# The last chunk's output product in three accumulators instead of one

## The chip, the cores and the metric

The kernel runs on one core of a Trainium2 chip. The metric is the time of one execution on the device in microseconds (us); the time of a kernel is the median of several runs. A profile is taken from one further execution. Its "span" is the time from the first to the last recorded instruction, and its own time is a little longer than its span.

## The reference

Per head, a 40x40 state is carried through 768 tokens, and each token reads it before it is updated. The 3072 rows that come out (4 batches of 768 tokens, 8 heads of 40 side by side make 320 columns) go through a feed-forward layer with a squared ReLU:

```python
for t in range(S):
    y[:, :, t] = einsum('bhd,bhde->bhe', rt, state)
    Sa = einsum('bhde,bhe->bhd', state, at)
    state = state * wt[:, :, None, :] - einsum('bhd,bhe->bhde', Sa, bt) + einsum('bhd,bhe->bhde', vt, kt)
x = y.transpose(0, 2, 1, 3).reshape(3072, 320)
h = x @ w_in                   # 320 -> 2048
g = maximum(h, 0) ** 2
out = g @ w_out                # 2048 -> 320
```

## The kernel before

**Chunks.** The 768 tokens are cut into 12 chunks of 64. For each chunk c the kernel loads its slices, prepares decay factors, solves the recurrence inside the chunk, carries the state on, reads it out, turns the result so that features lie on partitions (XT), and runs the feed-forward layer on the chunk's 4 x 64 = 256 rows. Matmul inputs are bf16; products are accumulated in PSUM as fp32.

**Feed-forward of one chunk (function ffn).** The hidden layer has 16 blocks of 128 features, handled in four groups u of four blocks. For each group the matmuls "F" and "FL" fill a PSUM tile, "f" applies the ReLU on its way to the SBUF buffer G (two buffers, chunk c uses G[c % 2]), and "q" squares it in place, on VectorE (DVE), ScalarE (ACT) or GpSimd (POOL). Then the output product "O" runs over the same 16 blocks j. The chunk's 256 rows are two row groups g of 128. For one j and one g, one matmul takes 128 columns of G as weights (128x128) and the 320 columns of WOUT[:, j] as moving data, and adds into columns 0 to 319 of half g of one PSUM tile. Each half is 512 fp32 wide. A chunk has 16 x 2 = 32 such matmuls, in four steps "O c u0" to "O c u3"; step u needs the squares of groups 0 to u.

**The ordinary chunk** is then copied out of PSUM to the SBUF buffer osb in one instruction ("o c", 128x640), and two DMAs on SyncE's queue (SP) store it, one for each pair of batches ("st c", line 947).

**The last chunk (c = 11)** is handled apart. Its last step u3 is split into "OL 11 g1" and "OL 11 g0": four matmuls for row group 1, then four for row group 0. Four copies follow, each 128x160: for g = 1 and then g = 0, columns 0 to 159 on ACT ("o0", line 374) and columns 160 to 319 on DVE ("o1", line 369). Four DMAs (line 960) store 63 rows each: for each g, one ("st0") on SP's queue and one ("st1") on ACT's queue. It has 63 rows instead of 64, since the output is shifted by one token.

**What sets the order.** A plan records every operation with what it reads and writes; the order itself is written out by hand in the string ORDER (lines 87 to 215), which names the engine, the PSUM slot (PE0 to PE3; four slots of two 2 KiB banks each) and the operation. Operations are issued in that order, each engine works its own queue in order, and the waits between engines are put in by the framework from the tiles and the regions that the instructions touch. The end of ORDER is:

```python
u3; ACT q 11 u3; PE2 O 11 u0; DVE o 10; PE O 11 u1; SP st 10; PE O 11 u2; PE OL 11 g1; PE OL 11
g0; ACT o0 11 g1; DVE o1 11 g1; ACT o0 11 g0; DVE o1 11 g0; ACT st1 11 g0; ACT st1 11 g1; SP st0
11 g1; SP st0 11 g0"""
```

In the instruction list of the kernel the waits of these last instructions are: the first copy (ACT, g1) waits for PE; each of the other three copies waits for the copy before it on the other engine, although it reads other columns; a store waits for the copies of its own g only. Line 388 is the helper that issues every ordinary matmul, line 395 the one for whole 128x128 transposes, lines 369 and 374 the copies on DVE and ACT; lines 908, 914, 916 and 918 are the ReLU on ACT and the squares on DVE, POOL and ACT; lines 947 and 960 are the output stores.

Of the kernel before, what the change touches and what calls it, by code (L numbers as in the profile page):

```python
# [7 lines left out]
FP32 = mybir.dt.float32  # L8
# [201 lines left out]
ACT f 10 u2; DVE f 10 u1; PE1 F 11 u2; ACT q 10 u2; DVE q 10 u1; PE0 FL 11 u1; PE2 FL 11 u3; DVE q  # L210
10 u0; PE FL 11 u2; PE FL 11 u0; PE F 11 u3; ACT f 11 u0; PE F 11 u1; ACT f 11 u2; PE3 O 10 u0;
ACT q 11 u2; PE O 10 u1; ACT f 11 u1; PE O 10 u2; ACT f 11 u3; POOL q 11 u1; ACT q 11 u0; PE O 10
u3; ACT q 11 u3; PE2 O 11 u0; DVE o 10; PE O 11 u1; SP st 10; PE O 11 u2; PE OL 11 g1; PE OL 11
g0; ACT o0 11 g1; DVE o1 11 g1; ACT o0 11 g0; DVE o1 11 g0; ACT st1 11 g0; ACT st1 11 g1; SP st0
11 g1; SP st0 11 g0"""


@with_exitstack
def kernel(
# [13 lines left out]
    NB, NHH, T, D = r.shape  # L233
    L = 64
    NCH = T // L
# [4 lines left out]
    DM = moe_w_in.shape[0]  # L240
# [85 lines left out]
    def slot(h, dt):  # L326

        if h not in slots:
            i = plan.slot_of[h]
            slots[h] = ps.tile([128, 2, 512 if dt == FP32 else 1024], dt, name=f"pb{i}",  # L330
                               tag=f"pb{i}", bufs=1)
        return slots[h]
# [8 lines left out]
    def pe(name, mode, cols, mms, **kw):  # L341

        d = {"R": max(28.6, cols / 2.4 + 1) / 2, "Q": max(31.0, cols / 2.4 + 1) / 2,
             "C": max(31.0, cols / 2.4 + 1) / 2,
             "D": max(22 if cols < 64 else 60.6, cols / 2.4 + 2.5)}[mode]
        plan.add(name, [("PE", d * len(mms))], ("pe", d, mms), mode=mode, n_mm=len(mms), **kw)

    def ew(name, alts, **kw):
        plan.add(name, [(e, d) for e, d, _ in alts], ("ew", {e: f for e, d, f in alts}), **kw)
# [14 lines left out]
    def copy_alts(o_, i_, n, fast=False, scale=None, engines=("DVE", "ACT")):  # L364
        alts = []
        if "DVE" in engines:
            if scale is None:
                alts.append(("DVE", c_dve(n, fast),
                             lambda: nc.vector.tensor_copy(out=o_(), in_=i_())))  # L369
            else:  # L370
                alts.append(("DVE", c_dve(n), lambda: nc.vector.tensor_scalar(  # L371
                    out=o_(), in0=i_(), scalar1=scale, scalar2=None, op0=ALU.mult)))
        if "ACT" in engines:
            alts.append(("ACT", c_act(n), lambda: nc.scalar.activation(  # L374
                out=o_(), in_=i_(), func=ACTF.Copy, scale=1.0 if scale is None else scale)))
        if "POOL" in engines:
            alts.append(("POOL", 190 + 0.83 * n,
                         lambda: nc.gpsimd.tensor_copy(out=o_(), in_=i_())))  # L378
        return alts
# [493 lines left out]
    def ffn(c):  # L873
        q2 = c % 2
        for u in range(NFB // 4):
            hf = ("F", c, u)
            tail = u % 2 == 1
            ms = []
            for rg in range(2):
                for i in range(2):  # L880
                    for k2 in range(2):
                        ms.append(mm(
                            lambda rg=rg, i=i, hf=hf: slot(hf, FP32)[:, rg, NT * i:NT * i + NT],
                            lambda rg=rg, k2=k2, i=i, u=u: WIN[
                                :, k2, 512 * u + 256 * rg + 128 * i:
                                512 * u + 256 * rg + 128 * i + 128],
                            lambda k2=k2: XT[q2][:, k2, :],
                            i == 0 and k2 == 0 and not tail, k2 == 1 and tail))
            wide = dict(reads=[("XT", q2), ("WIN", 0, u), ("WIN", 1, u)], writes=[hf],
                        alloc=[] if tail else [hf])  # L890
            ml = []
            for i in range(2):
                for rg in range(2):
                    ml.append(mm(
                        lambda rg=rg, i=i, hf=hf: slot(hf, FP32)[:, rg, NT * i:NT * i + NT],
                        lambda rg=rg, i=i, u=u: WLAST[
                            rows(rg), u, 128 * i:128 * i + 128],
                        lambda rg=rg: XT[q2][rows(rg), 2, :], i == 0 and tail, not tail))
            last = dict(reads=[("XT", q2), ("WLAST",)], writes=[hf], alloc=[hf] if tail else [])
            for x in (1, 0) if tail else (0, 1):  # L900
                if x:
                    pe(f"FL {c} u{u}", "R", NT, ml, **last)
                else:
                    pe(f"F {c} u{u}", "D", NT, ms, **wide)
            gv = G[q2][:, 4 * u:4 * u + 4, :].rearrange("p j t -> p (j t)")
            gb = G[q2][:, 4 * u:4 * u + 4, :].rearrange("p (s j) t -> p s (j t)", s=2)
            ew(f"f {c} u{u}", [
                ("ACT", c_act(1024), lambda gb=gb, hf=hf: nc.scalar.activation(  # L908
                    out=gb, in_=slot(hf, FP32)[:], func=ACTF.Relu)),
                ("DVE", c_dve(1024), lambda gb=gb, hf=hf: nc.vector.tensor_scalar(  # L910
                    out=gb, in0=slot(hf, FP32)[:], scalar1=0.0, scalar2=None, op0=ALU.max))],
               reads=[hf], writes=[("G", q2, u)], free=[hf])
            ew(f"q {c} u{u}", [
                ("DVE", 690, lambda gv=gv: nc.vector.tensor_tensor(
                    out=gv, in0=gv, in1=gv, op=ALU.mult)),
                ("POOL", 1900, lambda gv=gv: nc.gpsimd.tensor_tensor(  # L916
                    out=gv, in0=gv, in1=gv, op=ALU.mult)),
                ("ACT", c_act(1024), lambda gv=gv: nc.scalar.activation(  # L918
                    out=gv, in_=gv, func=ACTF.Square))],
               reads=[("G", q2, u)], writes=[("G", q2, u)])  # L920
        ho = ("O", c)
        for u in range(NFB // 4):
            ms = [[], []]
            for j in range(4 * u, 4 * u + 4):
                for g in range(2):
                    ms[g].append(mm(
                        lambda g=g: slot(ho, FP32)[:, g, 0:DM],
                        lambda g=g, j=j: G[q2][:, j, 2 * g * L:2 * g * L + 2 * L],
                        lambda j=j: WOUT[:, j, :], j == 0, j == NFB - 1))
            rd = ([("G", q2, x) for x in range(max(u, O_AFTER) + 1)]  # L930
                  + [("WOUT", 2 * u), ("WOUT", 2 * u + 1)])
            if c == NCH - 1 and u == NFB // 4 - 1:

                for g in range(2):
                    pe(f"OL {c} g{g}", "D", DM, ms[g], reads=rd, writes=[ho + (g,)])
            else:
                pe(f"O {c} u{u}", "D", DM, [m for x in zip(*ms) for m in x], reads=rd,
                   writes=[ho, ho + (0,), ho + (1,)], alloc=[ho] if u == 0 else [])
        ov = out.rearrange("(g bb s) f -> bb s g f", g=2, bb=2)
        t0, n = c * L + 1, min(L, T - 1 - c * L)  # L940
        if c < NCH - 1:
            ew(f"o {c}", copy_alts(lambda: osb[q2][:], lambda: slot(ho, FP32)[:, :, 0:DM], 2 * DM),
               reads=[ho, ho + (0,), ho + (1,)], writes=[("osb", q2)], free=[ho])

            def store():
                for bb in range(2):
                    nc.sync.dma_start(out=ov[bb, t0:t0 + n], in_=osb[q2][64 * bb:64 * bb + n])
            plan.add(f"st {c}", [("SP", 1500)], ("ew", {"SP": store}), reads=[("osb", q2)],
                     writes=[("left", c)])
            return  # L950
        h = DM // 2
        for g in range(2):
            for x, e in enumerate(("ACT", "DVE")):
                ew(f"o{x} {c} g{g}", copy_alts(
                    lambda g=g, x=x: osb[q2][:, g, h * x:h * x + h],
                    lambda g=g, x=x: slot(ho, FP32)[:, g, h * x:h * x + h], h, engines=(e,)),
                   reads=[ho + (g,), ("left", c - 2)], writes=[("osb", q2, g, x)], free=[ho])
            for bb, (e, q) in enumerate((("SP", nc.sync), ("ACT", nc.scalar))):
                plan.add(f"st{bb} {c} g{g}", [(e, 750 if e == "SP" else 60)],
                         ("ew", {e: lambda q=q, bb=bb, g=g: q.dma_start(  # L960
                             out=ov[bb, t0:t0 + n, g], in_=osb[q2][64 * bb:64 * bb + n, g])}),
                         reads=[("osb", q2, g, 0), ("osb", q2, g, 1)])

    def weights():

# [97 lines left out]
```

## Time and profile before

| | |
|---|---|
| median of 3 runs | 250.95 us (249.91 to 251.05) |
| the profiled execution's own time | 249.74 us |
| its span | 248.0 us |
| mean granted TensorE clock | 0.987 of full speed |
| TensorE (PE) busy | 223.8 us, 90% of the span |
| VectorE (DVE) busy | 189.1 us, 76% |
| ScalarE (ACT) busy | 178.0 us, 72% |
| GpSimd (POOL) busy | 110.1 us, 44% |

How to read the views used below. A row of a timeline has the start in us from the span's start, the length in us, the engine, the line, the operation, what it writes and reads, the count of instructions merged in it, and in brackets how long the engine had been idle and what released it. In the chain of waits each row is a piece of the one chain that ended last: start, length, engine and line. A row of the groups has the count, the busy time in us, the mean of one in ns, and the idle time before. PE is the matmul itself and PEld the weight load, which has a row of its own. SPq and ACTq are the issue of DMAs by those engines; a DMA's transfer goes on after its issue has ended. The page also cuts the span into 40 slices of 6.2 us; each digit is the busy share of a slice in tenths.

### The profile page before, as it was taken

The page shows a single profiled execution, that of the slowest core. Times are in us where ns is not written, and L with a number is a line of the kernel's source. Part 1 is how long each engine was busy: PE and PEld are TensorE (multiplying, and loading weights), DVE is VectorE, ACT ScalarE, POOL GpSimd, SP SyncE. Part 2 cuts the span into 40 slices and gives each one's busy share as a digit, 9 for nine tenths or more (in the row PEclk, how much of TensorE's full clock was granted, in tenths as well). Part 3 has the DMA queues.
Part 4 walks back from the last instruction along what each step waited for, and adds up shares of the span by engine and source line. Part 5 has one row for each costly group of instructions (what it writes and reads, how often), then busy time and mean ns, then how long its engine had stood idle before and what let it go on. Part 6 is the DMA issues. An engine that isn't in the chain of part 4 may idle for free.

```text
span 248.0 us, 12188 instructions
## 1 busy us (share of the span) xinstructions
PE 223.8 (90%) x5568; PEld 177.3 (71%) x5568; DVE 189.1 (76%) x236; ACT 178.0 (72%) x236; POOL 110.1 (44%) x110
## 2 busy tenths in 40 slices
PE   0588677599999999999999999999999999999991
PEld 0377666488787877788878877877788787867770
DVE  7698988359987889898869696999897578854411
ACT  2588889569899687868777887774777773944850
POOL 4144024532765716473870991491279900033030
PEclk9999999979999999999999999999999999999997
DMA  5989899989999969769698099995410000302021
GB/s 131 209 216 206 168 200 259 328 145 214 181 215 207 152 150 168 138 128 181 136 183 166 14 219 152 193 176 119 119 47 3 3 5 15 96 5 56 0 50 55
DMA packets 102152, 33.54 MB, mean 135 GB/s; under 512 B 88918, under 2 KB 101718, under 8 KB 101846
## 3 DMA queue, kind: packets, MB, share of 16 engines
q1 hardware_dynamic: 101958, 32.62, 63.0%
q8 instruction: 43, 0.70, 1.3%
q10 hardware_dynamic: 144, 0.16, 0.2%
q14 instruction: 7, 0.06, 0.1%
HBM read 28.84 MB, written 3.93 MB: 132 GB/s over the span
## 4 chain that ended last, share of the span: by engine, by line
PE 74%; DVE 9%; DMA 6%; ACT 4%; issue 3%; POOL 1%; SPq 1%; ACTq 0%
PE pb L388 63%; PE pb L392 7%; PE pb L395 4%; DMA G<-in_moe_w_in_dram 3%; DVE KBT L510 2%; DMA raw_a<-in_a_dram 2%; DVE AR L643 1%; DMA out_dram<-osb 1%; POOL WIN L378 1%; ACT G L908 1%; DVE STb L318 1%; DVE VU L371 1%; DVE lo L384 1%; DVE EN L669 1%; ACT osb L374 1%
## 5 line engine op out<-in xcount | busy, mean ns | idle before, releaser
L388 PE MATMUL pb<-WOUT,G 128*128 128x320 bf16 x384 | 57.1, 299 | 0.0
L916 POOL TENSOR_TENSOR G<-G 128x1024 bf16<-128x1024 bf16 x19 | 36.2, 1913 | 39.7 <-PE pb L392 19.3
L388 PE MATMUL pb<-XT,WIN 128*128 128x256 bf16 x384 | 49.9, 279 | 0.0
L908 ACT ACTIVATE G<-pb 128x1024 bf16<-128x1024 f32 x37 | 37.4, 1022 | 14.3 <-PE pb L388 13.1
L388 PEld LDWEIGHTS <-G 128*128 128x128 bf16 x384 | 35.9, 98 | 13.8 <-issue 0.5
L388 PEld LDWEIGHTS <-WIN 128*128 128x128 bf16 x384 | 35.6, 99 | 8.0 <-issue 2.6
L669 DVE TENSOR_TENSOR CX<-pb,MSKI 128x1024 bf16<-128x1024 f32 x24 | 28.9, 1220 | 12.1 <-PE pb L388 11.9
L382 POOL TENSOR_TENSOR KB<-raw_kb,iG 128x640 bf16<-128x640 f32 x14 | 21.6, 1542 | 24.3 <-ACT iG L553 19.9
L669 DVE TENSOR_TENSOR EN<-pb,MSK 128x1024 bf16<-128x1024 f32 x24 | 29.1, 1217 | 3.2 <-PE pb L388 3.1
L559 ACT ACTIVATE Gin<-pb 64x320 f32<-64x320 f32 x48 | 20.2, 428 | 9.4 <-PE pb L388 8.9
L378 POOL CAST VU<-raw_v 64x640 bf16<-64x640 f32 x20 | 14.3, 713 | 16.0 <-DMA raw_v<-in_v_dram 15.6
L761 DVE TENSOR_TENSOR STb<-pb,GT 64x640 bf16<-64x640 f32 x22 | 18.1, 820 | 1.4 <-PE pb L388 0.8
L388 PEld LDWEIGHTS <-EN 64*64 64x64 bf16 x768 | 14.5, 110 | 5.8 <-issue 4.8
L918 ACT ACTIVATE G<-G 128x1024 bf16<-128x1024 bf16 x17 | 17.7, 1055 | 0.1
L643 DVE TENSOR_TENSOR AR<-pb,GT 128x512 bf16<-128x512 bf16 x24 | 15.6, 683 | 2.7 <-PE pb L395 1.7
L374 ACT ACTIVATE osb<-pb 128x640 f32<-128x640 f32 (+1 forms) x10 | 6.2, 623 | 15.2 <-PE pb L388 14.7
L910 DVE TENSOR_SCALAR G<-pb 128x1024 bf16<-128x1024 f32 x11 | 13.4, 1222 | 4.7 <-PE pb L388 4.1
L388 PE MATMUL pb<-XT,WLAST 64*128 64x256 bf16 x192 | 16.8, 271 | 0.0
L382 POOL TENSOR_TENSOR lo<-lnW,hi 128x640 bf16<-128x640 f32 x6 | 8.9, 1492 | 15.8 <-ACT hi L374 10.3
L388 PE MATMUL pb<-hi,UTI 64*128 64x320 bf16 x48 | 7.9, 325 | 7.9 <-DVE hi L369 7.9
L839 DVE TENSOR_TENSOR Yb<-pb,Gin 128x128 bf16<-128x128 f32 (+1 forms) x24 | 12.4, 549 | 2.5 <-PE pb L388 2.3
L374 ACT ACTIVATE AR<-pb 128x512 bf16<-128x512 bf16 x19 | 10.6, 595 | 5.2 <-PE pb L392 3.6
(112 smaller groups left out, 447.1 us busy)
## 6 DMA issues: line engine op xcount, KB each, us to landing
raw_w<-in_w_dram SPq DMA_DIRECT2D x24, 160.0 KB, 4.3
raw_a<-in_a_dram SPq DMA_DIRECT2D x24, 160.0 KB, 4.1
raw_kb<-in_b_dram SPq DMA_DIRECT2D x24, 160.0 KB, 4.1
raw_kb<-in_k_dram SPq DMA_DIRECT2D x24, 160.0 KB, 4.2
raw_v<-in_v_dram SPq DMA_DIRECT2D x24, 160.0 KB, 5.4
raw_r<-in_r_dram SPq DMA_DIRECT2D x22, 160.0 KB, 5.2
out_dram<-osb SPq DMA_DIRECT2D x22, 160.0 KB, 3.1
osb<-in_moe_w_out_dram SPq DMA_DIRECT2D x8, 320.0 KB, 4.8
```

The source lines that it names most:

```text
L374: alts.append(("ACT", c_act(n), lambda: nc.scalar.activation(out=o_(), in_=i_(), func=ACTF.Copy, scale=1.0 if scale is None else scale)))
L378: lambda: nc.gpsimd.tensor_copy(out=o_(), in_=i_())))
L382: return [("POOL", 40 + 2.35 * n, lambda: nc.gpsimd.tensor_tensor(out=o_(), in0=a_(), in1=b_(), op=op)), ("DVE", c_dve(n), lambda: nc.vect ...
L388: return lambda: nc.tensor.matmul(out=o_(), lhsT=l_(), rhs=r_(), start=start, stop=stop, skip_group_check=True)
L392: return lambda: nc.tensor.transpose(out=o_(), in_=i_(), identity=IDb[rows(g), :])
L559: nc.scalar.activation(out=Gin[c % NGI][rows(g), NP * jh:NP * jh + NP, :].rearrange("p j e -> p (j e)"), in_=slot(hb, FP32)[rows(g), g, 0: ...
L643: ew(f"tA {c} g{g}", [("DVE", c_dve(512), lambda g=g: nc.vector.tensor_tensor(out=steps(AR[q2][:, 0, g]), in0=turned(ha, g), in1=steps(GT[ ...
L669: evac(f"m{nm} {c} g{g}", lambda s, n: [("DVE", c_dve(n), lambda: nc.vector.tensor_tensor(out=dst[q2][:, g, s].rearrange("p q i t -> p (q ...
L761: ew(f"s {c} q{q}", [("DVE", c_dve(2 * n), lambda q=q: nc.vector.tensor_tensor(out=STb[q2][rows(q), :, q, 0:D], in0=slot(hs, FP32)[rows(q) ...
L908: ("ACT", c_act(1024), lambda gb=gb, hf=hf: nc.scalar.activation(out=gb, in_=slot(hf, FP32)[:], func=ACTF.Relu)),
L916: ("POOL", 1900, lambda gv=gv: nc.gpsimd.tensor_tensor(out=gv, in0=gv, in1=gv, op=ALU.mult)),
L918: ("ACT", c_act(1024), lambda gv=gv: nc.scalar.activation(out=gv, in_=gv, func=ACTF.Square))],
```

## The change

Only the last chunk's output product, its copies, its stores and the end of ORDER are changed. Its 256x320 result is now held in three PSUM tiles: part A (row group 1, all 320 columns, slot 1), part B (row group 0, columns 0 to 159, slot 0) and part C (row group 0, columns 160 to 319, slot 2). Each part starts at column 0 of its own tile. So row group 0 has two matmuls of 160 columns for each block j, with the same weights loaded for each, where it had one of 320. There are three copies in place of four: A on DVE (128x320), B on ACT and C on DVE (128x160 each). The four stores are the same DMAs, but each g's two stores stand in ORDER right behind that g's last copy. On ACT the store of g1 now stands ahead of the copy of B.

The steps run in the order A B C for u0, A B C for u1, A for u2, A for u3, B C for u2, then B and C for u3:

```diff
-u3; ACT q 11 u3; PE2 O 11 u0; DVE o 10; PE O 11 u1; SP st 10; PE O 11 u2; PE OL 11 g1; PE OL 11
-g0; ACT o0 11 g1; DVE o1 11 g1; ACT o0 11 g0; DVE o1 11 g0; ACT st1 11 g0; ACT st1 11 g1; SP st0
-11 g1; SP st0 11 g0"""
+u3; ACT q 11 u3; PE1 OA 11 u0; DVE o 10; PE0 OB 11 u0; PE2 OC 11 u0; PE OA 11 u1; SP st 10; PE OB
+11 u1; PE OC 11 u1; PE OA 11 u2; PE OA 11 u3; PE OB 11 u2; PE OC 11 u2; DVE oa 11; SP st0 11 g1;
+ACT st1 11 g1; PE OB 11 u3; ACT ob 11; PE OC 11 u3; DVE oc 11; SP st0 11 g0; ACT st1 11 g0"""
...
+        parts = ((("A", 1, 0, DM), ("B", 0, 0, DM // 2), ("C", 0, DM // 2, DM))
+                 if c == NCH - 1 else ())
         for u in range(NFB // 4):
             ms = [[], []]
+            for p, g, x, y in parts:
+                hp = ho + (p,)
+                pe(f"O{p} {c} u{u}", "D", y - x, [
+                    mm(lambda hp=hp, x=x, y=y: slot(hp, FP32)[:, 0, 0:y - x],
+                       lambda g=g, j=j: G[q2][:, j, 2 * g * L:2 * g * L + 2 * L],
+                       lambda j=j, x=x, y=y: WOUT[:, j, x:y], j == 0, j == NFB - 1)
+                    for j in range(4 * u, 4 * u + 4)],
+                   reads=[("G", q2, x) for x in range(u + 1)]
+                   + [("WOUT", 2 * u), ("WOUT", 2 * u + 1)],
+                   writes=[hp], alloc=[hp] if u == 0 else [])
+            if parts:
+                continue
...
-        h = DM // 2
+        for p, g, x, y in parts:
+            ew(f"o{p.lower()} {c}", copy_alts(
+                lambda g=g, x=x, y=y: osb[q2][:, g, x:y],
+                lambda p=p, x=x, y=y: slot(ho + (p,), FP32)[:, 0, 0:y - x], y - x),
+               reads=[ho + (p,), ("left", c - 2)], writes=[("osb", q2, g, p)], free=[ho + (p,)])
         for g in range(2):
-            for x, e in enumerate(("ACT", "DVE")):
-                ew(f"o{x} {c} g{g}", copy_alts(
-                    lambda g=g, x=x: osb[q2][:, g, h * x:h * x + h],
-                    lambda g=g, x=x: slot(ho, FP32)[:, g, h * x:h * x + h], h, engines=(e,)),
-                   reads=[ho + (g,), ("left", c - 2)], writes=[("osb", q2, g, x)], free=[ho])
             for bb, (e, q) in enumerate((("SP", nc.sync), ("ACT", nc.scalar))):
                 plan.add(f"st{bb} {c} g{g}", [(e, 750 if e == "SP" else 60)],
                          ("ew", {e: lambda q=q, bb=bb, g=g: q.dma_start(
                              out=ov[bb, t0:t0 + n, g], in_=osb[q2][64 * bb:64 * bb + n, g])}),
-                         reads=[("osb", q2, g, 0), ("osb", q2, g, 1)])
+                         reads=[("osb", q2, g, p) for p, y, _, _ in parts if y == g])
```

In the changed kernel's instruction list, PE's queue is the same as before up to the last chunk's output product and has 16 more weight loads and 16 more matmuls in it; ACT, DVE and SP are the same up to the copies of the last chunk. Each of the three copies waits for PE and for earlier stores out of osb, and for no other copy. The stores of g1 wait for the copy of A, those of g0 for the copies of B and C.

More of the change, by code (lines that the diff above doesn't have):

```diff
@@ L931, in ffn @@
                   + [("WOUT", 2 * u), ("WOUT", 2 * u + 1)])
[L932 to L938, printed above, removed]
+            pe(f"O {c} u{u}", "D", DM, [m for x in zip(*ms) for m in x], reads=rd,
+               writes=[ho], alloc=[ho] if u == 0 else [])
         ov = out.rearrange("(g bb s) f -> bb s g f", g=2, bb=2)
@@ L942, in ffn @@
             ew(f"o {c}", copy_alts(lambda: osb[q2][:], lambda: slot(ho, FP32)[:, :, 0:DM], 2 * DM),
-               reads=[ho, ho + (0,), ho + (1,)], writes=[("osb", q2)], free=[ho])
+               reads=[ho], writes=[("osb", q2)], free=[ho])
             def store():
```

## Prediction

> **What bounds the kernel now.** I read the page's slices first: they tell which engine is full where the change is made.
>
> ```profile
> span 248.0 us, 12188 instructions
> ...
> PE   0588677599999999999999999999999999999991
> ...
> DVE  7698988359987889898869696999897578854411
> ACT  2588889569899687868777887774777773944850
> ...
> PEclk9999999979999999999999999999999999999997
> DMA  5989899989999969769698099995410000302021
> ```
>
> From slice 9 on PE is 90% or more busy until the last slice; in the last two DVE and ACT are nearly idle. So PE paces the kernel up to the last chunk's output product, and behind it comes a tail in which PE does nothing. The chain of waits, from 226 us on, shows what that tail is made of.
>
> ```profile
> 227.77 14.92 PE pb L388 x132
> 242.69 0.02 issue
> 242.71 0.31 ACT osb L374
> 243.03 0.02 issue
> 243.05 0.34 DVE osb L369
> 243.39 0.02 issue
> 243.41 0.31 ACT osb L374
> 243.72 0.02 issue
> 243.75 0.33 DVE osb L369
> ```
>
> PE runs without a gap to 242.69. Then four copies stand **one behind the other**, ACT, DVE, ACT, DVE, to 243.75 + 0.33 = 244.08. They read different columns, and those of row group 1 were complete four matmuls before PE ended; still the first starts behind the last matmul, and each other one behind the copy before it. The timeline of the same end names the releasers and shows the stores.
>
> ```profile
> 233.82 8.86 PE L388 MATMUL pb<-WOUT,G 128*128 128x320 bf16 x64
> ...
> 242.71 0.30 ACT L374 ACTIVATE osb<-pb 128x160 f32<-128x160 f32 x1 [3.80 <-PE pb L388]
> 243.05 0.32 DVE L369 COPY osb<-pb 128x160 f32<-128x160 f32 x1 [3.86 <-ACT osb L374]
> 243.40 0.98 SPq L960 DMA_DIRECT2D out_dram<-osb  x2
> 243.41 0.30 ACT L374 ACTIVATE osb<-pb 128x160 f32<-128x160 f32 x1 [0.39 <-DVE osb L369]
> 243.75 0.33 DVE L369 COPY osb<-pb 128x160 f32<-128x160 f32 x1 [0.37 <-ACT osb L374]
> 244.10 0.94 ACTq L960 DMA_DIRECT2D out_dram<-osb  x2
> ```
>
> DVE waits for ACT and ACT for DVE. SP's first store (g1) is issued at 243.40, as soon as its two copies are done; ACT's two at 244.10, behind all copies. The stores' issue times and the last wait of SP's queue:
>
> ```profile
> L960 SPq DMA_DIRECT2D out_dram<-osb x2: 288/294/301, 243.4 to 244.1; - x2
> L960 ACTq DMA_DIRECT2D out_dram<-osb x2: 288/453/618, 244.1 to 244.8; - x2
> ...
> SPq L1058 <- DMA out_dram<-osb: 2.6, 1, 2.6
> ```
>
> SP's second issue begins at 243.40 + 0.98 - 0.29 = 244.09 and ends at 244.38; then SP waits 2.6 us for a landing, to 246.98. ACT's pair spans 244.10 to 245.04, so its second store begins at 244.75 if the 0.62 us issue came first. Behind the wait there is 248.0 - 246.98 = 1.0 us of closing work, which I take as fixed, and the execution's own 249.74 is 1.7 us over the span.
>
> **The change part by part.**
>
> *PE.* Sixteen matmuls of 320 columns become thirty-two of 160, each with its own 128x128 weight load. The trace has no 160-column matmul. These rows bound it: the groups of O matmuls and of their weight loads, a group of whole transposes (the timeline, then its mean).
>
> ```profile
> L388 PE MATMUL pb<-WOUT,G 128*128 128x320 bf16 x64 | 8.9, 299 | 0.0
> ...
> L388 PEld LDWEIGHTS <-G 128*128 128x128 bf16 x384 | 35.9, 98 | 13.8 <-issue 0.5
> ...
> 70.57 1.06 PE L395 MATMUL pb<-IDQ,STb 128*128 128x128 bf16 x16
> ...
> L395 PE MATMUL pb<-IDQ,STb 128*128 128x128 bf16 x64 | 4.2, 219 | 0.8 <-DVE AR L643 0.8
> ```
>
> Back to back, a 320-column matmul follows the one before by (8.86 - 0.30) / 63 = 0.136 us, and a 128-column one, also with a 128x128 load each, by (1.06 - 0.22) / 15 = 0.056 us. The line through both, 0.417 ns per column plus 2.6 ns, gives 0.069 us for 160 columns. So the stream grows by 32 x 0.069 - 16 x 0.136 = **+0.04 us**. Bounds: 0 from below (the columns are the same) and, if a weight load could not go faster than one per 98 ns, 32 x 0.098 - 2.17 = +0.96 from above. I take +0.04, since 0.056 was reached with the same load.
>
> [...]
>
> *Does PE now wait for G?* The squares of the last chunk are on ACT and POOL.
>
> ```profile
> 236.19 1.89 POOL L916 TENSOR_TENSOR G<-G 128x1024 bf16<-128x1024 bf16 x1 [7.78 <-ACT G L908]
> 237.86 1.06 ACT L918 ACTIVATE G<-G 128x1024 bf16<-128x1024 bf16 x1
> ```
>
> The chunk's product starts at 233.82 + 32 x 0.136 = 238.17. Group 0 is squared by 237.86 (0.3 us ahead), group 1 by 238.08 and needed at 239.27, group 3 by 238.92 and needed at 240.91 (part A's u3; before, it was needed later). No wait is added. The slots 1 and 0 that A and B take are freed by ReLUs that ACT ran before the one that frees slot 2, so none is late.
>
> *The copies.* PE's order ends A u3, B u2, C u2, B u3, C u3, with 16 half-width matmuls (1.11 us) behind A. PE's end moves to 242.73, A is complete at 241.62, B at 242.45. Copy A is 128x320 on DVE, between two shapes in this row (min is 128x160, max 128x640):
>
> ```profile
> L369 DVE COPY osb<-pb x3: 324/325/824, 238.4 to 243.7; 128x160 f32<-128x160 f32 x2, 128x640 f32<-128x640 f32 x1
> ```
>
> 0.325 + 0.499 / 3 = 0.49 us: 241.65 to 242.14, beside PE. Then g1's two stores are issued at about 242.16. On ACT that store stands **ahead of copy B**: its issue takes 0.29 to 0.62 us, so ACT is free at 242.45 to 242.78. B is ready at 242.45, so its copy ends at 242.78 to 243.10. Copy C on DVE runs 242.76 to 243.09, waiting for PE alone. So both engines are done at about 243.10 and g0's pair is issued at **243.12**, where before the same pair was issued at 244.10, and one more store at 244.75. The ACT issue is hidden to within 0.02 us; each us that it took beyond 0.62 would move the end by a us.
>
> *The stores.* Four as before, on the same queues, in the other order on ACT. Behind the last copy stand two instead of three. How long until SP is released? Before: 246.98 - 244.10 = 2.88 us from the pair, 2.23 us from the last store. After, the pair is the last wave: 2.23 us from below if it goes as a last store does, 2.88 if the pair itself set the end and the third store cost nothing. I take 2.4, near the lower row, since the store that the pair shared the DMA engines with is gone, but the pair still starts at one moment. That releases SP at 245.5, **1.48 us earlier**; PE's +0.04 is in it. If ACT's second store is issued in 0.29 us instead of 0.62, up to 0.3 us more is gained.
>
> **Sum:** 249.74 - 1.5 = 248.25 us in the profiled execution's frame. The runs' median is 1.2 us above that execution; nothing here touches what makes them differ, so against the median it is 250.95 - 1.5 = **249.45 us**, I say 249.4. The bounds of the stores alone give a gain of 1.0 (2.88) to 1.65 (2.23), with the shorter issue 1.9.
>
> **The rivals**, all against the median.
>
> 1. *The weight load sets the pace* of the 160-column matmuls, 98 ns each: gain 1.5 - 0.92 = 0.6, 250.4 us. For it: the mean of 98 ns in the load's row, over the 69 ns that a matmul would take. Against: loads of that size at 56 ns apart. Chance 0.07.
> 2. *The landing sets the end.* Both queues issue at one moment, ACT's store takes the long issue again, and SP is released 2.88 us after the pair: gain 1.0, 249.95 us. For it: the 0.62 us issue on ACT began within 0.01 us of one on SP. Against: one store fewer in the last wave. Chance 0.18.
> 3. *The copies are still tied*, and the change doesn't do what it says: all three write the buffer osb, and if that tied them C would wait for B to 243.10 and end at 243.43, a gain of 1.5 - 0.33 = 1.15, 249.8 us. Against: in the instruction list copy C waits for PE, not for ACT; and before, SP's store of g1 went out at 243.40 while a copy into osb's other half began at 243.41. Chance 0.03.
> 4. *Slower: the load is not overlapped.* If each half-width matmul began only when its load had ended, one would take 0.098 + 0.068 = 0.166 us, the stream grows by 32 x 0.166 - 2.17 = 3.14 and the kernel is slower by 3.14 - 0.04 - 1.5 = 1.6 us: 252.55. It decides from (2.17 + 1.54) / 32 = 0.116 us per matmul. The 56 ns row speaks against it plainly. Chance 0.04.
>
> [...]
>
> **How the numbers follow.** The forecast has 0.68, the rivals 0.07, 0.18, 0.03 and 0.04. About 0.5% (1.25 us) is what a measurement of this kernel can tell from no change, and the runs of before spread over 1.1 us, so a true gain of 1.5 is measured as more than 1.25 only about four times in five. Faster by over 0.5%: 0.8 x 0.68 + 0.3 x 0.18 + 0.3 x 0.03 = 0.61; slower: 0.04; within: 0.35. The range, in the median's frame: the cheapest stores give 250.95 - 1.9 = 249.05, and the fastest run of before is 1.0 below the median: 248.0; above, rival 1 at 250.4 and 0.2 for the runs: 250.6.
>
> **What would show it.** In the profile after: O's rows of 160 columns 0.069 us apart; PE's end at 242.7; a DVE copy 128x320 before PE's end; ACT's and DVE's 128x160 copies side by side with PE named as releaser, both ended by 243.1; no copy that waits for a copy; SP's last wait over by 245.5 and a span near 246.5. I am wrong if half-width matmuls stand 0.08 us or more apart, if ACT's store issue holds copy B past 243.2, or if SP's wait ends more than 2.8 us behind the pair's issue.

## The result, and the profile after

| | before | after |
|---|---|---|
| median of 20 runs each | 251.17 us | 249.89 us |
| lowest run | 248.74 us | 247.81 us |
| ratio after / before, 95% interval | | 0.9946 [0.9922, 0.9971] |
| profiled execution: its own time / span | 249.74 / 248.0 us | 250.58 / 248.9 us |

The runs gained 0.54%, about 1.4 us (0.7 to 2.0 by the interval). Ratios here and below leave out executions that were set apart as slow (over 1.5% above the fastest of the same kernel), such as one of e2's four, at 418.83 us, and e6's profile is of one. Yet the profiled execution of after is longer than that of before. So the first thing to read is where the two profiles part. The page of after:

```profile
span 248.9 us, 12220 instructions
...
PE   0588779689999999999999999899999999999992
...
DVE  8697979769889779899859696799897678856411
ACT  2587869878698587878777897574678691952860
...
PEclk9999999979999999999999999999999999999998
DMA  5988999998898888879697189877240000402003
```

The slices have the same shape: PE full to the last one, DVE and ACT nearly idle at the end. The instructions up to the last chunk's product are the same, and still the copy of chunk 10's output, which stands just ahead of the change on DVE, starts 1.80 us later than in before (240.17 against 238.37). That is the spread of executions, not the change: in the second profiles below the order is reversed (240.89 in before, 238.94 in after). What the change can move lies behind it. The timeline of after's end (compare the six lines of before in the prediction):

```profile
237.79 6.72 PE L388 MATMUL pb<-WOUT,G 128*128 128x320 bf16 x64
...
240.17 0.82 DVE L369 COPY osb<-pb 128x640 f32<-128x640 f32 x1 [6.37 <-PE pb L388]
...
243.45 0.49 DVE L369 COPY osb<-pb 128x320 f32<-128x320 f32 x1 [2.46 <-DMA out_dram<-osb]
243.97 1.38 SPq L968 DMA_DIRECT2D out_dram<-osb  x2
243.97 0.63 ACTq L968 DMA_DIRECT2D out_dram<-osb  x1
244.55 0.33 DVE L369 COPY osb<-pb 128x160 f32<-128x160 f32 x1 [0.62 <-PE pb L388]
244.72 0.30 ACT L374 ACTIVATE osb<-pb 128x160 f32<-128x160 f32 x1 [4.01 <-PE pb L388]
245.06 0.30 ACTq L968 DMA_DIRECT2D out_dram<-osb  x1
```

PE ends at 237.79 + 6.72 = 244.51. Copy A lies beside PE, copies B and C beside each other, and both name PE as releaser: the chain of four is gone. But copy B on ACT starts 0.21 us behind PE's end, not before it: ahead of it on ACT stands the store of row group 1, 243.97 to 244.60. The profile puts copy A's wait to a DMA; the copy waits for several semaphores, among them those of earlier stores out of the same buffer, and a timeline of PE alone, from 243.4 to 244.6, shows when A was complete:

```profile
243.11 1.41 PE L388 MATMUL pb<-WOUT,G 128*128 128x320 bf16 x17
```

These are A's last matmul, started at 243.11, and the 16 half-width ones. With the 0.30 us that a 320-column matmul takes A is complete at 243.41, 0.04 before the copy. SP's waits close the execution:

```profile
SPq L1066 <- DMA out_dram<-osb: 2.5, 2, 2.3
```

SP's second store of the last chunk ends at 243.97 + 1.38 = 245.35; 2.5 us later SP is released, at 247.85, and 1.0 us of closing work follows. I measure the change from here on by the **tail**: from the end of PE's last matmul to the end of the span (the trace gives the two spans as 248.03 and 248.88). It is 248.03 - 242.69 = 5.34 us before and 248.88 - 244.51 = 4.37 after, **0.97 us less**, or 0.39%, inside the interval of the ratio. Sums of rounded rows like these are good to about 0.02 us.

### The profile page after: what moved, and what is told of

It reads as the page before. It is cut to its first block, busy times and chain, and to the rows that moved or that the text cites. A ratio compares the mean times of both kernels' runs of the same rounds, so it can differ in the third digit from the quotient of the medians.

```text
span 248.9 us, 12220 instructions
## 1 busy us (share of the span) xinstructions
PE 224.5 (90%) x5584; PEld 179.2 (72%) x5584; DVE 191.4 (77%) x236; ACT 177.4 (71%) x235; POOL 110.8 (45%) x110
## 3 DMA queue, kind: packets, MB, share of 16 engines
HBM read 28.84 MB, written 3.93 MB: 132 GB/s over the span
## 4 chain that ended last, share of the span: by engine, by line
PE 72%; DVE 9%; DMA 7%; ACT 5%; issue 4%; POOL 1%; SPq 1%; ACTq 0%
PE pb L388 61%; PE pb L392 7%; PE pb L395 4%; DMA G<-in_moe_w_in_dram 3%; DMA raw_a<-in_a_dram 2%; DMA out_dram<-osb 2%; DVE KB L384 1%; DVE KBT L510 1%; DVE AR L643 1%; POOL WIN L378 1%; ACT G L908 1%; DVE STb L318 1%; DVE VU L371 1%; DVE STb L761 1%; ACT VU L374 1%
## 5 line engine op out<-in xcount | busy, mean ns | idle before, releaser
L388 PE MATMUL pb<-WOUT,G 128*128 128x320 bf16 (+1 forms) x400 | 57.1, 294 | 0.0
L388 PE MATMUL pb<-XT,WIN 128*128 128x256 bf16 x384 | 48.3, 273 | 0.0
L388 PEld LDWEIGHTS <-G 128*128 128x128 bf16 x400 | 36.6, 98 | 13.3 <-issue 0.5
L388 PEld LDWEIGHTS <-WIN 128*128 128x128 bf16 x384 | 34.9, 98 | 7.3 <-issue 2.6
L382 POOL TENSOR_TENSOR KB<-raw_kb,iG 128x640 bf16<-128x640 f32 x14 | 22.2, 1582 | 25.8 <-ACT iG L553 20.6
L553 ACT ACTIVATE iG<-pb 128x640 f32<-128x640 f32 x18 | 12.4, 696 | 2.5 <-PE pb L388 2.4
```

Of the source, the lines that this page charges most:

```text
L382: return [("POOL", 40 + 2.35 * n, lambda: nc.gpsimd.tensor_tensor(out=o_(), in0=a_(), in1=b_(), op=op)), ("DVE", c_dve(n), lambda: nc.vect ...
L388: return lambda: nc.tensor.matmul(out=o_(), lhsT=l_(), rhs=r_(), start=start, stop=stop, skip_group_check=True)
```

## The experiments

My theory after the result: the copies' chain was the cost, and the tail is now the issue of the last pair of stores, then their landing, then 1.0 us. The rival: the landing of the stores sets the end however early the copies are done. The first four kernels, run together, take these apart; each edit is against after unless said otherwise.

**e1: two accumulators.** Row group 0 is whole again; no half-width matmuls.

```diff
-        parts = ((("A", 1, 0, DM), ("B", 0, 0, DM // 2), ("C", 0, DM // 2, DM))
+        parts = ((("A", 1, 0, DM), ("B", 0, 0, DM))
...
-ACT st1 11 g1; PE OB 11 u3; ACT ob 11; PE OC 11 u3; DVE oc 11; SP st0 11 g0; ACT st1 11 g0"""
+ACT st1 11 g1; PE OB 11 u3; DVE ob 11; SP st0 11 g0; ACT st1 11 g0"""
```

> Two accumulators, one for each row group, both copied by DVE (128x320 each); no 160-column matmuls. Measured as the tail, from the end of PE's last matmul to the end of the span: 5.35 us before, 4.37 after. If what the change bought is that the copies are untied from each other and that row group 1 is copied early, the halving of row group 0 is worth little: the last copy takes 0.49 instead of 0.33 but waits for no store on ACT, the last pair of stores is issued 0.53 us behind PE's end (after: 0.55), tail 4.3 to 4.5, and PE is 0.04 us shorter. Rival: the two half-width copies on two engines are what pays; then the tail is 0.16 us or more longer than after's, 4.55 or above.

Ratio to before 0.9960 [0.9920, 1.0000]. Timeline of e1's end:

```profile
237.81 3.97 PE L388 MATMUL pb<-WOUT,G 128*128 128x320 bf16 x28
...
241.25 1.37 SPq L968 DMA_DIRECT2D out_dram<-osb  x2
241.25 1.38 ACTq L968 DMA_DIRECT2D out_dram<-osb  x2
241.81 0.49 DVE L369 COPY osb<-pb 128x320 f32<-128x320 f32 x1 [0.59 <-PE pb L388]
```

PE ends at 241.78, the pair is issued at 242.33, 0.55 us behind, and the span ends at 246.15: tail 4.37, as after. The halving of row group 0, with one half on ACT, bought nothing (with both halves on DVE, e5 below, the tail is 0.04 shorter); what paid is that row group 1 has a tile of its own and that no copy waits for a copy.

**e2: row group 1's stores both on SP.**

```diff
-ACT st1 11 g1; PE OB 11 u3; ACT ob 11; PE OC 11 u3; DVE oc 11; SP st0 11 g0; ACT st1 11 g0"""
+SP st1 11 g1; PE OB 11 u3; ACT ob 11; PE OC 11 u3; DVE oc 11; SP st0 11 g0; ACT st1 11 g0"""
...
-            for bb, (e, q) in enumerate((("SP", nc.sync), ("ACT", nc.scalar))):
+            for bb, (e, q) in enumerate((("SP", nc.sync), ("ACT", nc.scalar) if g == 0
+                                         else ("SP", nc.sync))):
```

> As after, but row group 1's store on ACT's queue goes on SP's queue, so nothing stands ahead of copy B on ACT. If that store's issue is what delayed copy B, B starts within 0.05 us of its last matmul's end and the last pair is issued 0.39 us behind PE's end instead of 0.55. ACT's only store is then its first: if the long issue of 0.62 us belongs to the first store on a queue, it comes back here at the end of the chain, and the tail is 4.4 to 4.6; if it belongs to the moment after a copy or to another cause that is gone, the issue takes 0.29 us and the tail is 4.2.

Ratio 0.9899 [0.9819, 0.9978], from three executions only. Its end:

```profile
237.79 4.55 PE L388 MATMUL pb<-WOUT,G 128*128 128x320 bf16 x48
...
242.10 0.30 ACT L374 ACTIVATE osb<-pb 128x160 f32<-128x160 f32 x1 [3.56 <-PE pb L388]
242.38 0.32 DVE L369 COPY osb<-pb 128x160 f32<-128x160 f32 x1 [0.61 <-PE pb L388]
242.79 0.58 ACTq L969 DMA_DIRECT2D out_dram<-osb  x1
```

Copy B now starts 0.24 us **before** PE's end (242.34), and SP issues its last store at 242.77, 0.43 behind it, ACT its own at 0.45: the store on ACT was what held B. ACT's only store takes the long issue, 0.58 us; in after the first took 0.63 and the second 0.30, although both began at the same moment as one on SP. So with stores of 63 rows the long issue, 0.58 to 0.64 us in these profiles, goes with the first one on ACT's queue. (In e6 and e7, where the stores are cut, it is the second that is long: 0.40 and 0.41 us for the first, of 48 rows, then 0.72 and 0.70 for one of 15.) Tail 4.27, 0.10 less. The 4.4 to 4.6 expected for the case that the long issue comes back is a miss: SP is released 2.8 us behind the pair, as in after.

**e3: before with one copy** of 128x640 in place of the four.

```diff
-g0; ACT o0 11 g1; DVE o1 11 g1; ACT o0 11 g0; DVE o1 11 g0; ACT st1 11 g0; ACT st1 11 g1; SP st0
+g0; DVE o 11; ACT st1 11 g0; ACT st1 11 g1; SP st0
...
```

> Before, with its one accumulator and its order on PE, but one DVE copy of 128x640 in place of the four chained ones, and the four stores behind it. If the chain of copies was what cost, its 1.40 us become 0.84 and the stores start 0.55 us earlier: first store 0.87 us behind PE's end, last one on ACT 1.5 to 1.55 behind it (before: 2.07), tail 4.8 to 4.95. Rival: the landing of the four stores sets the end whatever the copies do; then the two stores of row group 1, which before went out 0.7 us ahead, now share the DMA engines with the others and the tail stays at 5.2 to 5.4.

Ratio 0.9991 [0.9946, 1.0037]. Its end:

```profile
237.76 5.46 PE L388 MATMUL pb<-WOUT,G 128*128 128x320 bf16 x39
...
243.26 0.82 DVE L369 COPY osb<-pb 128x640 f32<-128x640 f32 x1 [3.52 <-PE pb L388]
244.11 0.67 SPq L956 DMA_DIRECT2D out_dram<-osb  x2
244.12 0.95 ACTq L956 DMA_DIRECT2D out_dram<-osb  x2
```

PE ends at 243.22, the first store is issued at 244.11 (0.89 behind), the span ends at 248.27: tail 5.05, between the two expectations. The copies gave back 0.52 us, but from the first of the four stores to the end it takes 4.16 us. So the landing does take a part of what the copies give.

**e4: a lone last store** (ACT's last store left out).

```diff
-ACT st1 11 g1; PE OB 11 u3; ACT ob 11; PE OC 11 u3; DVE oc 11; SP st0 11 g0; ACT st1 11 g0"""
+ACT st1 11 g1; PE OB 11 u3; ACT ob 11; PE OC 11 u3; DVE oc 11; SP st0 11 g0"""
...
```

> After, without ACT's store of row group 0: 63 rows of one batch in the last chunk are left out of the output. One store stands behind the last copy. After: SP is released 2.79 us behind the issue of the last pair. If the two stores of the pair slow each other on the DMA engines, the lone one lands 1.75 to 2.1 us behind its issue and the tail is 3.3 to 3.7. Rival: a store has its 2.8 us alone too, as a fixed delay; then the tail stays at 4.3.

SP's last wait in e4:

```profile
SPq L1066 <- DMA out_dram<-osb: 1.6, 1, 1.6
```

The store is issued at 243.12 and SP's wait for it ends at 245.08, 1.95 us behind the start of the issue, against 2.79 in after. Tail 3.52. So 2.8 us is not the delay of a store by itself: the second store of the last pair is worth **0.85 us** of the tail.

**e5: copy B on DVE,** so that ACT only issues stores.

```diff
-ACT st1 11 g1; PE OB 11 u3; ACT ob 11; PE OC 11 u3; DVE oc 11; SP st0 11 g0; ACT st1 11 g0"""
+ACT st1 11 g1; PE OB 11 u3; DVE ob 11; PE OC 11 u3; DVE oc 11; SP st0 11 g0; ACT st1 11 g0"""
```

> After, with copy B on DVE instead of ACT, so that all three copies are on DVE and ACT only issues stores. If the store ahead of copy B on ACT cost 0.16 us, that is won back: DVE copies A, then B (ready 0.28 us before C), then C without a wait for ACT, and the last pair is issued 0.41 us behind PE's end (after: 0.55; with both of row group 1's stores on SP: 0.39); ACT's last store is its second and is issued in 0.30 us. Tail 4.2 to 4.25 (after: 4.37). Rival: two engines are needed for the two halves; then copy C starts late behind B on DVE and the pair is issued at 0.6 or later.

Ratio 0.9970 [0.9932, 1.0008]. Its end:

```profile
233.77 8.63 PE L388 MATMUL pb<-WOUT,G 128*128 128x320 bf16 x78
...
241.84 1.23 SPq L968 DMA_DIRECT2D out_dram<-osb  x2
241.85 1.24 ACTq L968 DMA_DIRECT2D out_dram<-osb  x2
242.15 0.60 DVE L369 COPY osb<-pb 128x160 f32<-128x160 f32 x2 [0.34 <-PE pb L388]
```

The pair is issued at 242.78, 0.38 us behind PE's end (242.40), 0.17 earlier than in after, as expected; but from the pair to the end of the span it takes 3.95 us instead of 3.81. Tail 4.33: a miss by 0.1. The earlier pair mostly waited longer: 0.96 us from issue to first packet, in after 0.82 (see e11).

**e6: each store cut into 48 and 15 rows.**

```diff
+                def store(q=q, bb=bb, g=g):
+                    for i, m in ((0, 48), (48, n)):
+                        q.dma_start(out=ov[bb, t0 + i:t0 + m, g],
+                                    in_=osb[q2][64 * bb + i:64 * bb + m, g])
...
```

> After, with each store of 63 rows cut into one of 48 and one of 15 rows. The lone store showed that the two of the last pair slow each other (2.79 us to SP's release, 1.96 alone). If that is because a store of 63 rows is spread over few DMA engines, whole multiples spread it over more, the last wave lands 0.3 to 0.5 us sooner behind its issue; against it, ACT now issues two stores ahead of copy B, which delays the pair by 0.1 to 0.3 us. Tail 4.0 to 4.3. Rival: it is the number of stores in flight that counts; then four in the last wave take longer than two and the tail is 4.5 or more.

Ratio 0.9957 [0.9901, 1.0013]. Now two stores stand ahead of copy B on ACT and hold it longer:

```profile
235.55 8.90 PE L388 MATMUL pb<-WOUT,G 128*128 128x320 bf16 x80
...
243.91 1.15 ACTq L969 DMA_DIRECT2D out_dram<-osb  x2
...
245.18 0.30 ACT L374 ACTIVATE osb<-pb 128x160 f32<-128x160 f32 x1 [4.53 <-DVE osb L369]
245.51 0.86 ACTq L969 DMA_DIRECT2D out_dram<-osb  x2
```

The last stores are issued 1.06 us behind PE's end (244.45), 0.5 later than in after; still the tail is 4.32, since they take only 3.26 us to the end of the span. Two effects of half a us cancel: the pair was held by 0.5 us where 0.1 to 0.3 was expected, so the tail just misses its range, and the rival's 4.5 is out.

**e7: both** (copy B on DVE, stores cut).

> Both edits: copy B on DVE and stores cut into 48 and 15 rows. If the two causes are separate, the tail is 3.75 to 3.95: the pair issued 0.41 us behind PE's end, the last wave landing 2.3 to 2.5 us behind that. Rival, as in the run before: with four stores in the last wave it is 4.3 or more. The time against before would be lower by 1.4 to 1.6 us in the first case.

The end of e7 (four stores on each queue):

```profile
239.34 1.41 PE L388 MATMUL pb<-WOUT,G 128*128 128x320 bf16 x17
...
240.19 1.72 SPq L969 DMA_DIRECT2D out_dram<-osb  x4
240.20 2.11 ACTq L969 DMA_DIRECT2D out_dram<-osb  x4
```

Tail 244.53 - 240.75 = **3.78**, as the first theory expected. The time: median 248.47 us against 250.37, ratio 0.9942 [0.9906, 0.9977]. The DMA rows of after's last 5 us (243.9 to 248.9) and of a window as long in e7 (240.0 to 245.0), in slices of 0.125 us, show the difference:

```profile
DMA  0000002556365631455655310000000000000000
GB/s 0 0 0 0 0 0 61 143 102 123 102 195 184 246 113 41 143 195 174 174 195 184 103 21 20 31 20 10 0 0 0 0 0 0 0 0 0 0 0 0
```

```profile
DMA  0000000057989633653764530000000000000000
GB/s 10 0 0 0 0 0 0 0 123 154 226 287 236 175 82 82 184 154 123 205 195 144 133 72 10 0 0 0 0 0 0 0 0 0 0 0 0 0 0 0
```

In after the share of the 16 DMA engines stays below 7 tenths (0.51 in the mean from 245.9 to 246.8; nine engines of sixteen are 0.56), and the last wave ends with some 0.6 us at 10 to 31 GB/s (the share is 0.07 from 246.8 to 247.3, about one engine of sixteen). In e7 the share reaches 9 tenths and that end is missing. The trace's semaphore events, which the views do not list, go with this: as a store lands, its semaphore rises nine times for 63 rows, sixteen for 48 and fifteen for 15 (a store of 63 or 15 rows has one more rise ahead of these, in after 0.45 to 0.72 us behind the start of its issue). So do the packets under 512 B: after's four stores have 36 in the window above, 4 x 9, and e7's eight have 124 from 240.1 to 244.6, 4 x (16 + 15). Why the row counts differ so, no run shows.

**e8: after once more.**

> The changed kernel once more, for a second profile and more runs. If the tail is what the change changed, it is 4.3 to 4.45 again whatever the span is, and the ratio to before lies at 0.9945 to 0.9975 (0.6 to 1.4 us). Rival: the gain of the first comparison (1.4 us) holds and the tail of one profile understates it; then the second tail is shorter than 4.1.

Ratio 0.9977 [0.9939, 1.0015], tail 4.37 again. The expectation held for the tail; the ratio lies 0.0002 above its range. The first interval and this one both hold 0.9961, which is what 0.97 us would be; neither could tell 1.0 from 1.5 us, and this one alone could not tell the change from none.

**e9: the last pair on one queue,** SP's, in after.

```diff
-ACT st1 11 g1; PE OB 11 u3; ACT ob 11; PE OC 11 u3; DVE oc 11; SP st0 11 g0; ACT st1 11 g0"""
+ACT st1 11 g1; PE OB 11 u3; ACT ob 11; PE OC 11 u3; DVE oc 11; SP st0 11 g0; SP st1 11 g0"""
...
-            for bb, (e, q) in enumerate((("SP", nc.sync), ("ACT", nc.scalar))):
+            for bb, (e, q) in enumerate((("SP", nc.sync), ("ACT", nc.scalar) if g == 1
+                                         else ("SP", nc.sync))):
```

> After, with both stores of the last pair on SP's queue; ACT issues row group 1's store only. After: pair issued at one moment on two queues, SP released 2.79 us behind. If the two stores are slow together because they use the same few DMA engines, one queue changes little: the second is issued 0.3 us behind the first and SP is released 2.7 to 3.0 us behind the first one's issue, tail 4.3 to 4.5. Rival: two queues taking turns on an engine is what costs; then the first store lands as the lone one did, the second 0.3 to 0.5 us later, and the tail is 3.8 to 4.0.

The timeline of e9's end, then SP's last wait:

```profile
234.99 8.90 PE L388 MATMUL pb<-WOUT,G 128*128 128x320 bf16 x80
...
243.34 1.75 SPq L969 DMA_DIRECT2D out_dram<-osb  x3
```

```profile
SPq L1067 <- DMA out_dram<-osb: 1.7, 1, 1.7
```

PE ends at 243.89. SP's issues end at 245.09, so the pair begins at about 244.45 (0.56 behind), and SP is released at 246.8, **2.35 us** behind it, though the second store is issued 0.3 us later than on two queues. Tail 4.01, next to the rival's 3.8 to 4.0 and well under the 4.3 to 4.5 of the shared engines (there is one execution, and no ratio). My explanation by shared engines alone fell: from one queue the same two stores land sooner, 2.35 us behind their issue instead of 2.79, with the share of the DMA engines again below 7 tenths. The DMA rows of e9, 243.2 to 248.2:

```profile
DMA  0000000355555561345455532000000000000000
GB/s 0 0 0 0 0 0 0 102 154 113 102 143 185 215 225 41 92 133 154 143 184 205 174 113 82 21 0 0 0 0 0 0 0 0 0 0 0 0 0 0
```

The slow end is gone but for one slice. The semaphore events show what the slow end was. In after the eighth rise comes 2.11 us (SP's store of the last pair) and 2.31 us (ACT's) behind the issue, the ninth only at 2.62 and 2.80. In e9 the ninth comes at 2.01 and 2.03, 0.13 us at most behind the eighth. So in after one share of nine is half a us late in both stores.

What e9 does not settle is whether the queue counts or the moment: its second store is issued 0.34 us behind the first. In e3 the last two stores, on two queues but issued 0.32 us apart, have their ninth rise only 0.06 and 0.08 us behind the eighth.

**e10: before once more.**

> The kernel before once more, for a second profile of it. If the end behind PE's last matmul is the same from run to run, the tail is 5.25 to 5.45 again (5.34 in the first profile), with the four copies one behind the other, whatever the span is. Rival: the tail varies by as much as the spans do, by a us or more; then the comparison of tails between single profiles says nothing.

The span is 250.6 us, 2.6 more than in the first profile; PE ends at 236.34 + 8.86 = 245.20 and the tail is 5.39. So the tail repeats to 0.05 us where the span does not.

**e11: copy B on DVE and the last pair on SP.** The edit against e9:

```diff
-ACT st1 11 g1; PE OB 11 u3; ACT ob 11; PE OC 11 u3; DVE oc 11; SP st0 11 g0; SP st1 11 g0"""
+ACT st1 11 g1; PE OB 11 u3; DVE ob 11; PE OC 11 u3; DVE oc 11; SP st0 11 g0; SP st1 11 g0"""
```

> After, with copy B on DVE and the last pair of stores on SP's queue. Copy B on DVE alone gave a pair issued at 0.38 us behind PE's end, but a landing 2.93 behind it (tail 4.33); one queue alone gave 2.36 (tail 4.01). If it is the taking of turns of two queues that lengthens the last landing, the tail here is 3.7 to 3.85. Rival: the landing is bounded by what the stores of row group 1 leave in the DMA engines, and an earlier pair waits the longer; then the tail stays at 3.95 to 4.05. Time against before lower by 1.3 to 1.7 us.

Tail 4.12 (PE's end 240.35, span 244.47): neither. The pair is issued 0.40 us behind PE's end, 0.16 sooner than in e9, and needs 3.72 us to the end of the span instead of 3.45. Ratio 0.9984 [0.9953, 1.0015], which is 0.4 us where 1.3 to 1.7 was expected. As between after and e5, sending the pair earlier brought nothing or next to nothing.

The record shows why. These are the DMA rows of e5 in the window that stands to PE's end as after's does under e7 (241.78 to 246.78):

```profile
DMA  0000002456456531555654300000000000000000
GB/s 0 0 0 0 0 0 61 133 113 123 113 174 225 215 113 41 154 184 184 174 205 164 113 21 20 20 31 0 0 0 0 0 0 0 0 0 0 0 0 0
```

Slice by slice they are nearly after's rows: the dip between the stores of row group 1 and the last pair stands in the same slice, though the pair was issued 0.17 us sooner. In the trace's DMA packets the last pair's first one starts 1.35 to 1.37 us behind PE's end in after, e5, e9 and e11 alike, and the last one of row group 1's stores ends at 1.37 to 1.38. From issue to first packet it is 0.82 us in after, 0.96 in e5 and 0.98 in e11. So the pairs that were sent sooner waited for row group 1's stores to get through. The rival had the mechanism, with a tail 0.07 too short.

**e12: two accumulators and the last pair on SP.** The edit against e1 (with e9's choice of queue):

```diff
-ACT st1 11 g1; PE OB 11 u3; DVE ob 11; SP st0 11 g0; ACT st1 11 g0"""
+ACT st1 11 g1; PE OB 11 u3; DVE ob 11; SP st0 11 g0; SP st1 11 g0"""
...
```

> Two accumulators, one copy for each row group, both on DVE, and the last pair of stores on SP's queue: no 160-column matmuls and no copy on ACT. Two accumulators alone had a tail of 4.37 like after. If the pair's two queues cost 0.4 us there too, the tail is 3.9 to 4.05, and this simpler form is as good as three accumulators with one queue (4.01). Rival: the gain of one queue belongs to the wait for ACT's copy; then the tail stays at 4.3 or more.

Tail 4.03, as expected, with a pair issued 0.57 us behind PE's end. Ratio 0.9973 [0.9936, 1.0010].

All tails, and what they consist of (us):

| kernel | PE's end to first store of the last wave | from there to the span's end | tail |
|---|---|---|---|
| before / once more | 1.41 / 1.42 | 3.93 / 3.97 | 5.34 / 5.39 |
| e3, before with one copy | 0.89 | 4.16 | 5.05 |
| after / once more | 0.55 / 0.54 | 3.81 / 3.83 | 4.37 / 4.37 |
| e1, two accumulators | 0.55 | 3.82 | 4.37 |
| e2, group 1's stores on SP | 0.43 | 3.84 | 4.27 |
| e5, copy B on DVE | 0.38 | 3.95 | 4.33 |
| e6, stores cut | 1.06 | 3.26 | 4.32 |
| e9, last pair on SP | 0.56 | 3.45 | 4.01 |
| e12, two accumulators, last pair on SP | 0.57 | 3.46 | 4.03 |
| e11, B on DVE, last pair on SP | 0.40 | 3.72 | 4.12 |
| e7, B on DVE, stores cut | 0.39 | 3.39 | 3.78 |
| e4, lone last store | 0.54 | 2.98 | 3.52 |

(The first store of e3's wave is the first of four. Each kernel that was not run again has one profile.)

## Why the prediction was right, and where its sum was off

The time, 249.89 us, lies in the range, and the mechanism was right: the chained copies were the cost and are gone. The size was off. The tail gained 0.97 us, not 1.5, and the first ratio's 1.4 us stands for anything from 0.7 to 2.0. That the 1.4 fell so close to the forecast 1.5 is luck: the same comparison made again (e8) gives 0.6 us. The range also held rivals 1, 2 and 3 (250.4, 249.95 and 249.8), so the time alone spoke against none of them; the profiles had to (items 1, 4 and 5).

1. **PE, +0.04 us: right.** The 16 half-width matmuls and the one ahead take 1.41 us: (1.41 - 0.14 - 0.23) / 15 = 0.069 us each, with 0.23 us for one by their row in after's groups:

```profile
L388 PE MATMUL pb<-WOUT,G 128*128 128x160 bf16 x32 | 2.7, 233 | 0.0
```

   From chunk 10's copy to PE's end it takes 4.34 us, before 4.32. So rivals 1 (0.098) and 4 (0.166) are out.
2. **No wait for G: right.** There is no gap in PE's stream.
3. **Copies: right in kind, 0.16 us too early.** A at 1.06 us before PE's end (forecast 1.08), C at 0.04 behind it. The step that failed is "the ACT issue is hidden to within 0.02 us": the issue took 0.63, not 0.62, but 0.12 us passed between its end and copy B, and the store began only 0.54 before PE's end, so the pair went out at 0.55 instead of 0.39. e2 and e5 take the store, or the copy, off ACT and have 0.43 and 0.38. That delay cost little of the tail (0.10 and 0.04).
4. **Stores: the mis-sized term.** "I take 2.4, near the lower row, since the store that the pair shared the DMA engines with is gone": it measured 2.79. Rival 2, the landing at 2.88 and a gain of 1.0, is what the profile shows, though not by its reason: ACT's issue was short (0.30). e4 shows 0.85 us of the tail to be the pair's second store, and in e9 sending the pair from one queue, the second store 0.34 us later, is worth 0.36.
5. **Rival 3 is out:** copy B (244.72 to 245.02) ran beside copy C (244.55 to 244.88) into the same buffer.

The forecast of 1.48 less 0.16 for the later pair and 0.39 for the landing is 0.93, against 0.97 measured.

What stays open: why two queues leave one engine's worth of traffic to the end (a share of 0.07 from 246.8 to 247.3 in after), and whether the queues or the common moment of issue do it. In after's last half us of traffic the packets of the two queues alternate, one about every 0.05 us. That their taking turns is what makes the end late, no run shows, nor why one share of nine is behind the others.

Of the versions, e7 has the shortest full tail, 0.59 us under after's, and beats before clear of noise; its interval overlaps that of after in the same comparison (0.9942 against 0.9977), so that it beats after in time is not shown.

## What to carry to other kernels

At the end of this kernel nothing was left to hide the copies and the stores behind. In such a place, add up the copies that are tied to each other, then the issue and landing of the last stores, and look at which of the two ends last before giving a gain to the first. A tile for each part that is finished early is enough (two were as good as three here); then try the last stores from one queue, or cut into other row counts, here 48 and 15 for 63 (0.36 and 0.55 us of the tail), and see whether earlier stores are still moving before sending them sooner. Where the spread of executions is larger than the change, measure it in the profile from an event just ahead of it.

## What the runs showed of the hardware

- The first store on ACT's queue took 0.58 to 0.64 us to issue in every kernel with stores of 63 rows where ACT had one, the second 0.29 to 0.30. With stores of 48 and then 15 rows (e6, e7), the first took 0.40 to 0.41 and the second 0.70 to 0.72.
- Two stores of 63 rows issued at once on two queues released SP 2.8 us behind their issue (after, e1; 2.9 in e5), from one queue 2.4 (e9, e12; 2.6 in e11), a lone one 1.95 (e4).
- A store of 63 rows raised its semaphore nine times as it landed, one of 48 rows sixteen times, one of 15 rows fifteen times. In after the ninth rise came 0.5 us behind the eighth for both stores of the last pair.
- In e5 and e11 the last pair's first DMA packet started where row group 1's last one ended, 1.35 to 1.37 us behind PE's end, 0.96 and 0.98 us behind its issue.
- The part of the execution ahead of the change varied by about 5 us between fourteen profiles (chunk 10's copy started between 236.00 and 240.89), the tail of a kernel that was profiled twice by 0.05 us at most.
